# Sharing out one tensor's zeros among the transfer engines: another split of rows over GpSimd's and SP's transfers

## The chip, the cores and the metric

The kernel runs on one core of a Trainium2 chip. A core has TensorE for matrix products (PE; its weight loads are PEld), VectorE (DVE), ScalarE (ACT), GpSimd (POOL) and SyncE (SP), and sixteen transfer engines (DMA engines) that move data between the chip's memory and the core's SBUF, which has 128 partitions. The metric is the device time of one execution in microseconds. The kernel before took 272.31 us, the median of 3 runs (272.19 to 272.38).

## The reference

One decoding step of a transformer layer with its gradients: `x + attention(layernorm(x)) + ffn(layernorm(x))` for 4 batch rows with one token each, model width 512. The attention has 32 query heads and 8 key/value heads of 128; it looks only at the last `W = 1024` of `Sk = 4096` cached positions. The feed-forward part has a gate, an up and a down matrix with inner width 1792.

```python
xn = _layernorm(x)
k = k_cache[:, :, Sk - W:, :]        # each head used by 4 query heads; v likewise
p = softmax(einsum("bhqd,bhkd->bhqk", q, k) * Dh ** -0.5)
out = x + (p @ v).reshape(...) @ wo + (gelu(xn @ w_gate) * (xn @ w_up)) @ w_down
```

Nine outputs are wanted: `out`, and the gradients of x, of the two caches, and of five weight matrices, all in bf16. The gradients of the caches (out_2 and out_3) have the caches' full shape, 4 x 8 x 4096 x 128. Only the last 1024 positions of each head depend on the input; the first 3072 positions (`K0`) are zero, and the kernel has to write those zeros: 64 heads of 3072 x 128 elements, 50 MB of the 81 MB that it writes.

## The kernel before

**Zeros.** A tile `ztile` of 128 partitions by 6144 bf16 elements (12,288 bytes a partition, `ZW`) is set to zero once by GpSimd. A head's zero part is cut into 64 pieces (`ZP`) of 6144 elements, so that one row of `ztile` fills one piece. `zeros(n)` issues n transfers on SP's queue; each writes the zero parts of two heads (`ZG = 2`) with 128 pieces, from every other partition of `ztile`, 1.5 MB. There are 32 such pairs. A transfer of `zeros` waits for the one issued four earlier to have landed (`behind`, `deep=4`).

**One pair is written otherwise.** The last pair is taken off the list (`zog, zb, zg`) and written by `part_zeros`, with transfers that GpSimd issues. `part_zeros(m0, rows, each, part, after)` writes pieces m0 to m0 + rows * each of both heads. Its source has `rows` rows of `ztile`, the first in partition `part`; each row is read `2 * each` times. Three such transfers are issued while the second feed-forward weight gradient is prepared in program order; on GpSimd they come right behind a few fills, among the weight loads. They hold 15, 2 and 15 of the 64 positions. A fourth, with the other 32, is issued at the beginning of the last phase and waits for the zeros that SP issued last before it (`zdone[-1]`).

**Order of the work.** The weights come first, on SP's queue: gate, up, down, wq and wo. Then the feed-forward part and its gradients, then four rounds of attention, one for each batch row, then the last phase with the gradients of wo and wq, out and the gradient of x. SP's instructions stand in the order of the program (a `manual_schedule` for its engine); from the attention on TensorE, VectorE and ScalarE do too. GpSimd's instructions are placed by the scheduler, by what they depend on. SP's queue carries the loads, the results (`result`, from staging tiles) and the zeros, between which a list (`before`) says how many zeros go ahead of each result. SP's transfers use eight semaphores in turn, and each transfer waits for the one that used its semaphore before it, eight transfers back.

**Around the change.** After the feed-forward part SP issues the load of va, two zeros, the load of kb and four zeros.

Of the kernel before, what the change touches and what calls it, by code (L numbers as in the profile page):

```python
# [19 lines left out]
def kernel(  # L20
# [24 lines left out]
    nc = tc.nc  # L45
# [7 lines left out]
    K0 = Sk - W  # L53
# [29 lines left out]
    def evac(out, in_, n):  # L83

        ca, cd = (190 + n) / 1.2, (130 + n) / 0.96
        eng = "act" if load["act"] + ca <= load["dve"] + cd else "dve"
        load[eng] += ca if eng == "act" else cd
        if eng == "act":
            return nc.scalar.copy(out=out, in_=in_)  # L89
        return nc.vector.tensor_copy(out=out, in_=in_)  # L90

    def t32(out, in_, n):
        load["dve"] += (130 + n) / 0.96
        nc.vector.transpose(out=out, in_=in_)  # L94

    def pairs(ap):
        return ap.bitcast(U32)

    def scratch():
        return scrp.tile([P, 1024], U32, name="scr", tag="scr")  # L100
# [6 lines left out]
    def stg_tile():  # L107

        if not halves:
            pair = stg_pair()  # L110
            halves.extend(pair[:, h] for h in range(2))
        return halves.pop(0)
# [3 lines left out]
    def result(*parts):  # L116
        zeros(min(before.popleft(), len(ztodo)))
        for out, in_ in parts:
            nc.sync.dma_start(out=out, in_=in_)
# [19 lines left out]
    def mm(out, lhsT, rhs, first=True, last=True, pos=None):  # L139
        kw = {} if pos is None else {"tile_position": pos}  # L140
        nc.tensor.matmul(out, lhsT=lhsT, rhs=rhs, start=first, stop=last, **kw)  # L141

    def bank(name, tag="w", shape=(P, 512), dt=FP32):
        pool = {"w": ps_w, "x": ps_x}.get(tag, ps_a)
        return pool.tile(list(shape), dt, name=name, tag=tag)
# [75 lines left out]
    ZP = P // 2  # L221
    ZW = K0 // ZP * Dh
    ztile = const.tile([P, ZW], BF16, name="ztile")
# [36 lines left out]
    def window(dram, b, h):  # L260

        return dram[b, h * G // 2:(h + 1) * G // 2, K0:Sk, :].rearrange("g (m j) d -> m g (j d)", j=2 * J)

    def alternate(tl, h):

        t_ = tl[h:h + 1]
        return bass.AP(tensor=t_.tensor, offset=t_.offset,
                       ap=[[2 * t_.ap[0][0], P // 2], [2 * J * Dh, G // 2], [1, 2 * J * Dh]])

    def load_kv(b, k, pool, tag, eng, **kw):  # L270
        d_, src = ((k_t, A_k_cache), (v_t, A_v_cache))[k]
        tl = pool.tile([P, G // 2, 2 * J, Dh], BF16, name=tag, tag=tag)
        for h in range(2):
            with tc.high_priority():
                d = eng.dma_start(out=alternate(tl, h), in_=window(src, b, h), **kw)
        d_[b] = tl
        return d

    ZG = 2
    zsrc = bass.AP(tensor=ztile.tensor, offset=ztile.offset, ap=[[2 * ztile[:].ap[0][0], ZP], [0, ZG], [1, ZW]])  # L280
    ztodo = [(og, b, g) for b in range(B) for g in range(0, G, ZG) for og in (out_2, out_3)]
    zdone = []
    zog, zb, zg = ztodo.pop()

    def part_zeros(m0, rows, each, part, after=None):

        z = nc.gpsimd.dma_start(  # L287
            out=zog[zb, zg:zg + ZG, 0:K0, :].rearrange("g (m j) d -> m g (j d)", m=ZP)[m0:m0 + rows * each],
            in_=bass.AP(tensor=ztile.tensor, offset=ztile[part:part + 1, :].offset,
                        ap=[[4 * ztile[:].ap[0][0], rows], [0, ZG * each], [1, ZW]]))  # L290
        if after is not None:
            behind(z.ins, after.ins)

    def behind(ins, other):
        tc.add_manual_dep(ins, other.name,
                          mybir.DependencyInfo(mybir.DependencyClass.Sync, mybir.DependencyReason.DATA))

    def zeros(n, after=None, deep=4):

        for _ in range(n):  # L300
            og, b, g = ztodo.pop(0)
            z = nc.sync.dma_start(out=og[b, g:g + ZG, 0:K0, :].rearrange("g (m j) d -> m g (j d)", m=ZP), in_=zsrc)
            if len(zdone) >= deep:
                behind(z.ins, zdone[-deep].ins)
            if after is not None:
                behind(z.ins, after.ins)
            zdone.append(z)


    if True:  # L310
# [5 lines left out]
        def flat(t_):  # L316
            return t_[:].rearrange("p f c -> p (f c)")
# [92 lines left out]
        for wi, (wsb, dh, og) in enumerate(((wu_sb, dhu, out_7), (wg_sb, dhg, out_6))):  # L410
            dh_f = flat(dh)
            dhr = hgu[:].rearrange("p u f c -> p (u f c)").bitcast(BF16)
            for a, q in enumerate(quad):
                ps = bank("rep_ps", "w", (P, FQ))
                mm(ps[:], rsum_b[q, :], dh_f[q, :], pos=(Q * a, 0))
                evac(dhr[:, a * FQ:(a + 1) * FQ], ps[:], FQ)
            dhP = scratch()[:, 0:FPB * Q].rearrange("p (f x) -> p f x", f=FPB)
            t32(dhP, pairs(dhr[:, 0:F]), 896)
            dhs = ffn.tile([P, FPB, 2, 4 * B], BF16, name="dhs", tag=f"dhs{wi}")
            nc.gpsimd.memset(dhs[:], 0.0)  # L420
            if wi == 1:
                part_zeros(0, 3, 5, 0)
                part_zeros(15, 2, 1, 12)
                part_zeros(17, 3, 5, 20)
            dhPb = dhP.bitcast(BF16).rearrange("p f (x r) -> p f r x", r=2)
            for a, q in enumerate(quad):
                nc.vector.tensor_copy(out=dhs[q, :, :, a * B:(a + 1) * B], in_=dhPb[q, :, :, 0:B])
            for ch in range(4):
                sc = scratch()
                n7 = FPB // 4  # L430
                t32(sc[:, 0:n7 * P].rearrange("p (k c n) -> p c k n", k=n7, c=C),
                    pairs(wsb[:])[:, :, ch * n7 * Q:(ch + 1) * n7 * Q], 896)
                sb = sc[:, 0:n7 * P].bitcast(BF16).rearrange("p (k n r) -> p k r n", k=n7, r=2)
                for k in range(n7):
                    c = nm % 4
                    mm(dxf_ps[quad[c]].rearrange("p r n -> p (r n)"), dhs[:, ch * n7 + k].rearrange("p r x -> p (r x)"),
                       sb[:, k], nm < 4, nm >= 2 * FPB - 4, (0, Q * c))
                    nm += 1
            dwg_v = og.rearrange("(p h c) f -> h p (c f)", h=2, c=2)
            for h in range(2):  # L440
                stg = stg_tile()
                for ci in range(2):
                    for a, q in enumerate(quad):
                        ps = bank("dwg_ps", "w", (P, FQ))
                        mm(ps[:], xn_b[q, 2 * h + ci:D:C], dh_f[q, :], pos=(Q * a, 0))
                        o_ = (ci * NQ + a) * FQ
                        evac(stg[:, o_:o_ + FQ], ps[:], FQ)
                result((dwg_v[h], stg[:, 0:2 * F]))
# [4 lines left out]
    with tc.tile_pool(name="mid", bufs=1, reuse_waits="tile") as mid:  # L453
# [4 lines left out]
        with (tc.tile_pool(name="kvp", bufs=1, reuse_waits="tile") as kvp,  # L458
              tc.tile_pool(name="att", bufs=1, reuse_waits="tile") as att):
            load_kv(0, 1, kvp, "va", nc.sync)  # L460
            zeros(2)
            load_kv(1, 0, kvp, "kb", nc.sync)
            zeros(4)


# [2 lines left out]
            rows = [qm[:], dyBD[:].rearrange("p n r x -> p (n r x)").rearrange("p (b g d) -> p b g d", b=B, g=4)]  # L468
# [132 lines left out]
            def small(name, shape=(P, 1)):  # L601
                return att.tile(list(shape), FP32, name=name, tag=name)
# [72 lines left out]
            for b in range(B):  # L675
                S = sps[0][:]
                m = small("m")
# [124 lines left out]
            for i in range(KH):  # L802
                t, e, c = i // 8, i // 4 % 2, i % 4
# [12 lines left out]
            s_o = sums[:, 0:D]  # L816
            TT(out=s_o, in0=ob_ps[:], in1=fo[:], op=ALU.add)

            part_zeros(32, 8, 4, 64, zdone[-1])
            dwo_v = out_5.rearrange("(p t k) n -> t p (k n)", t=4, k=8)  # L820
            dwq_v = out_4.rearrange("(p c) j -> c p j", c=C)
            late = {}
# [126 lines left out]
```

## Time and profile before

| | |
|---|---|
| median of 3 runs | 272.31 us (272.19 to 272.38) |
| the profiled execution | 272.15 us |
| its span, first to last instruction | 270.4 us |
| DVE / PE / ACT / POOL busy | 67% / 61% / 51% / 13% of the span |
| last computation ends | about 243 us |
| moved | 111.9 MB, 414 GB/s over the span |
| HBM read, written | 30.7 MB, 81.0 MB |

Busy shares are of the span. A digit in a line of slices is the busy share of a fortieth of the span in tenths (9 is 90% or more). Queue q1 holds what SP issues, q0 what GpSimd issues. In the issues by line the columns are the target and source, the issuing engine, how many, the size of each, and the median time from issue to landing. The trace also has a record of every packet that a transfer engine moved: its queue, its size, its start and how long it took.

### The profile page before, as it was taken

How to read it: one execution, taken by the hardware profiler on the slowest of the kernel's cores; microseconds unless marked ns; L12 is line 12 of the kernel's file. 1: busy time of each engine (PE TensorE's matmuls, PEld its weight loads, DVE VectorE, ACT ScalarE, POOL GpSimd, SP SyncE). 2: the span in 40 equal slices, each digit the busy share in tenths (PEclk: the TensorE clock that was granted, in tenths of full speed). 3: DMA queues.
4: the chain of work that ended last, by engine and by line, in shares of the span. 5: the costliest groups of instructions: out<-in, count | busy, mean ns of one | idle time of the engine just before them, and what ended most of it. 6: DMA issues, size and time to landing. Idle time of an engine off the chain costs nothing.

```text
span 270.4 us, 3304 instructions
## 1 busy us (share of the span) xinstructions
PE 164.6 (61%) x1152; PEld 62.0 (23%) x1159; DVE 180.5 (67%) x339; ACT 137.4 (51%) x278; POOL 36.1 (13%) x95
## 2 busy tenths in 40 slices
PE   1256988968536687676568578585877898460000
PEld 0121342222112342123222233122421223010000
DVE  7869768978798428873588536793289999970000
ACT  2242775670022636696577765696476666460000
POOL 8900002091032101120012100000000000000000
PEclk9998885556855555997999975997577999555555
DMA  7999999999999999999999999999999999999994
GB/s 264 437 422 449 409 369 425 430 431 413 421 426 428 430 412 425 426 421 427 415 421 418 433 416 421 431 422 431 418 428 425 422 429 417 429 429 428 428 420 207
DMA packets 16640, 111.90 MB, mean 414 GB/s; under 512 B 1760, under 2 KB 1776, under 8 KB 10992
## 3 DMA queue, kind: packets, MB, share of 16 engines
q1 hardware_dynamic: 16072, 110.12, 97.7%
q0 software_dynamic: 544, 1.57, 1.5%
q8 instruction: 9, 0.15, 0.2%
q14 instruction: 7, 0.06, 0.1%
q10 hardware_dynamic: 8, 0.00, 0.0%
HBM read 30.68 MB, written 81.01 MB: 413 GB/s over the span
## 4 chain that ended last, share of the span: by engine, by line
DVE 21%; PE 21%; ACT 17%; issue 4%; ACTq 0%
DVE scr L94 9%; ACT stg L124 6%; ACT spr L584 5%; PE kv_ps L141 4%; PE dw_ps L141 4%; DVE stg L124 3%; PE sc_ps L141 3%; PE ok_ps L141 2%; DVE odt L647 2%; PE od_ps L141 2%; ACT late L124 2%; DVE dqs L763 2%; DVE wq_t L94 2%; PE ob_ps L141 1%; ACT last L124 1%
## 5 line engine op out<-in xcount | busy, mean ns | idle before, releaser
L124 ACT CAST stg<-kv_ps 128x512 bf16<-128x512 f32 x102 | 54.6, 598 | 26.5 <-PE kv_ps L141 26.4
L141 PE MATMUL sc_ps<-scr,bd 128*32 128x256 bf16 x256 | 20.1, 399 | 18.1 <-DVE scr L94 17.5
L141 PEld LDWEIGHTS <-spr 128*128 128x128 bf16 x256 | 17.0, 108 | 36.1 <-issue 24.3
L141 PE MATMUL kv_ps<-dyBD,spr 128*128 128x512 bf16 x60 | 24.1, 528 | 1.9 <-issue 1.3
L141 PE MATMUL kv_ps<-qm,spr 128*128 128x512 bf16 x63 | 19.7, 387 | 3.0 <-DVE stg L124 1.1
L94 DVE STREAM_TRANSPOSE scr<-va 128x1024 uint32<-128x1024 uint32 x16 | 19.5, 1224 | 0.0
L124 DVE CAST stg<-kv_ps 128x512 bf16<-128x512 f32 x10 | 6.6, 688 | 17.9 <-PE kv_ps L141 17.9
L89 ACT CAST stg<-dwg_ps 128x448 bf16<-128x448 f32 x26 | 12.0, 567 | 3.3 <-DMA out_dram<-stg 2.4
L549 POOL COPY bd<-D3q 32x64 bf16<-32x64 bf16 x32 | 7.6, 245 | 44.4 <-PE sc_ps L141 43.2
L141 PEld LDWEIGHTS <-bd 128*32 128x32 bf16 x256 | 6.3, 99 | 29.8 <-issue 27.2
L141 PE MATMUL dw_ps<-scr,xn_b 32*128 32x512 bf16 x32 | 9.4, 545 | 5.5 <-ACT late L124 4.0
L124 ACT CAST late<-dw_ps 128x512 bf16<-128x512 f32 x16 | 9.2, 588 | 6.8 <-PE dw_ps L141 6.7
L141 PE MATMUL do_ps<-scr,dyBD 128*128 128x512 bf16 x31 | 11.1, 491 | 2.3 <-DVE scr L94 1.9
L584 ACT ACTIVATE spr<-dS_b,amask 64x256 bf16<-64x256 bf16 x16 | 7.4, 554 | 8.5 <-DVE dS_b L728 8.5
L549 POOL COPY bd<-D3d 32x64 bf16<-32x64 bf16 x32 | 7.4, 239 | 31.7 <-PE sc_ps L141 16.4
L647 DVE SCALAR_TENSOR_TENSOR odt<-od_ps,om,odt 128x128 f32<-128x128 f32 x12 | 4.2, 351 | 11.1 <-ACT odt L642 10.8
L124 DVE CAST stg<-dw_ps 128x512 bf16<-128x512 f32 x16 | 10.5, 685 | 1.5 <-PE dw_ps L141 1.3
L287 POOL DMA_DIRECT2D out_dram<-ztile x4 | 3.0, 753 | 61.9 <-DMA out_dram<-ztile 61.9
L94 DVE STREAM_TRANSPOSE scr<-wo_sb 128x1024 uint32<-128x1024 uint32 x8 | 9.8, 1237 | 1.6 <-PE do_ps L141 1.0
L124 ACT CAST stg<-dw_ps 128x512 bf16<-128x512 f32 x16 | 8.9, 588 | 3.6 <-PE dw_ps L141 3.4
L94 DVE STREAM_TRANSPOSE scr<-ka 128x1024 uint32<-128x1024 uint32 x8 | 9.8, 1233 | 1.2 <-PE r_ps L141 1.1
L124 DVE CAST late<-dw_ps 128x512 bf16<-128x512 f32 x16 | 10.4, 675 | 0.3 <-PE dw_ps L141 0.3
(203 smaller groups left out, 337.4 us busy)
## 6 DMA issues: line engine op xcount, KB each, us to landing
out_dram<-ztile SPq DMA_DIRECT2D x31, 1536.0 KB, 19.1
out_dram<-stg SPq DMA_DIRECT2D x18, 1024.0 KB, 14.7
va<-in_A_v_cache_dram SPq DMA_DIRECT2D x8, 1024.0 KB, 14.3
out_dram<-stg SPq DMA_DIRECT2D x6, 896.0 KB, 11.9
wq_sb<-in_A_wq_dram SPq DMA_DIRECT2D x1, 4096.0 KB, 27.9
wo_sb<-in_A_wo_dram SPq DMA_DIRECT2D x1, 4096.0 KB, 37.3
ka<-in_A_k_cache_dram SPq DMA_DIRECT2D x4, 1024.0 KB, 15.6
kb<-in_A_k_cache_dram SPq DMA_DIRECT2D x4, 1024.0 KB, 19.0
```

The costliest lines, as they stand in the source:

```text
L89: return nc.scalar.copy(out=out, in_=in_)
L94: nc.vector.transpose(out=out, in_=in_)
L124: return nc.scalar.copy(out=out, in_=in_) if eng == "act" else nc.vector.tensor_copy(out=out, in_=in_)
L141: nc.tensor.matmul(out, lhsT=lhsT, rhs=rhs, start=first, stop=last, **kw)
L287: z = nc.gpsimd.dma_start(out=zog[zb, zg:zg + ZG, 0:K0, :].rearrange("g (m j) d -> m g (j d)", m=ZP)[m0:m0 + rows * each], in_=bass.AP(ten ...
L549: nc.gpsimd.tensor_copy(out=t_[q, :, :, g2, :, o_:o_ + 4], in_=src[q, b, g2])
L584: nc.scalar.activation(out=out, in_=in_, func=ACT.Copy, scale=amask[q, a:a + 1])
L647: STT(out=t_[:], in0=ps[:, g, :], scalar=(om, oms)[k][:, g:g + 1], in1=t_[:], op0=ALU.mult, op1=ALU.add)
L763: nc.vector.tensor_copy(out=dqs[q, :, :, :, a * B + b], in_=d3v[q])
```

## The change

The two heads that GpSimd wrote with 15 + 2 + 15 positions early and 32 late are split another way. GpSimd writes 5 positions from 5 rows (one position each), and 32 from 8 rows (4 each), issued where the three transfers were. In the last phase there are two `part_zeros` in place of one: 12 positions from 3 rows that start in partition 104, with the same wait as before, and 12 from 3 rows that start in partition 0, with no wait given. Rows of the source now lie eight partitions apart instead of four. The last 3 positions of both heads are written by SP, in a new function `rest_zeros`: 16 rows of 2304 elements, from one partition in eight, issued behind the load of kb. The target is written through a view (`zpart`) with the head as its outer dimension.

```diff
+    zpart = zog[zb, zg:zg + ZG, 0:K0, :].rearrange("g (m j) d -> g m (j d)", m=ZP)
+
     def part_zeros(m0, rows, each, part, after=None):
 
         z = nc.gpsimd.dma_start(
-            out=zog[zb, zg:zg + ZG, 0:K0, :].rearrange("g (m j) d -> m g (j d)", m=ZP)[m0:m0 + rows * each],
+            out=zpart[:, m0:m0 + rows * each].rearrange("g m e -> m g e"),
             in_=bass.AP(tensor=ztile.tensor, offset=ztile[part:part + 1, :].offset,
-                        ap=[[4 * ztile[:].ap[0][0], rows], [0, ZG * each], [1, ZW]]))
+                        ap=[[8 * ztile[:].ap[0][0], rows], [0, ZG * each], [1, ZW]]))
         if after is not None:
             behind(z.ins, after.ins)
+
+    def rest_zeros(m0):
+
+        n = (ZP - m0) * ZW // 8
+        nc.sync.dma_start(out=zpart[:, m0:ZP].rearrange("g m e -> g (m e)").rearrange("g (k e) -> g k e", k=8),
+                          in_=bass.AP(tensor=ztile.tensor, offset=ztile.offset, ap=[[8 * ztile[:].ap[0][0], 16], [1, n]]))
...
             if wi == 1:
-                part_zeros(0, 3, 5, 0)
-                part_zeros(15, 2, 1, 12)
-                part_zeros(17, 3, 5, 20)
+                part_zeros(0, 5, 1, 0)
+                part_zeros(5, 8, 4, 40)
...
             load_kv(1, 0, kvp, "kb", nc.sync)
+            rest_zeros(61)
             zeros(4)
...
-            part_zeros(32, 8, 4, 64, zdone[-1])
+            part_zeros(37, 3, 4, 104, zdone[-1])
+            part_zeros(49, 3, 4, 0)
```

## The prediction

> **What bounds the kernel now.** The page's slices come first, for the share of time in which the 16 transfer engines move data.
>
> ```profile
> DMA  7999999999999999999999999999999999999994
> GB/s 264 437 422 449 409 369 425 430 431 413 421 426 428 430 412 425 426 421 427 415 421 418 433 416 421 431 422 431 418 428 425 422 429 417 429 429 428 428 420 207
> DMA packets 16640, 111.90 MB, mean 414 GB/s; under 512 B 1760, under 2 KB 1776, under 8 KB 10992
> q1 hardware_dynamic: 16072, 110.12, 97.7%
> q0 software_dynamic: 544, 1.57, 1.5%
> ```
>
> The engines are full in all but the first and last slice. Then the table by stage (length, busy time of PE, PEld, DVE, ACT and POOL, granted clock, DMA share, GB/s):
>
> ```profile
> 42.00:100.00 58.00, 39.43 (x258) 14.62 (x252) 43.49 (x72) 23.08 (x48) 15.48 (x43) 0.56 1.01 425
> 100.00:200.00 100.00, 68.78 (x541) 29.11 (x545) 63.86 (x133) 67.06 (x143) 7.96 (x32) 0.83 1.02 423
> 200.00:243.00 43.00, 32.80 (x205) 8.78 (x204) 40.52 (x66) 28.54 (x54) 0.65 (x1) 0.81 1.02 426
> 243.00:266.00 23.00, 0.00 (x0) 0.00 (x0) 0.00 (x0) 0.00 (x0) 0.00 (x0) 0.50 1.00 424
> ```
>
> From 243 us nothing computes any more and the transfers need another 26 us. The end is that of the transfer engine that finishes last. So the question is what each engine has to move. The issues by line show the changed transfers:
>
> ```profile
> out_dram<-ztile SPq DMA_DIRECT2D x31, 1536.0 KB, 19.1
> out_dram<-ztile POOLq DMA_DIRECT2D x1, 768.0 KB, 11.9
> out_dram<-ztile POOLq DMA_DIRECT2D x2, 360.0 KB, 25.1
> out_dram<-ztile POOLq DMA_DIRECT2D x1, 48.0 KB, 21.9
> ```
>
> The packet records of the trace have no engine number. I chained each packet to the one that begins as it ends (within some 4 ns), backward from the last one, holding each chain to the order in which SP's queue must come. It gives 16 chains without an idle stretch over 0.3 us back to 30 us. The transfers that use only some engines name them: x, out_0 and out_1 (four rows) use engines 0 to 3; GpSimd's four take the engines in turn, as many as they have source rows: 0-2, 3-4, 5-7 and 8-15. Packets of 12,288 B (one piece) per engine and the end of its last packet:
>
> - engines 0-2: 10 pieces, 267.2 to 267.6 us
> - engine 3: 2 pieces, 265.1
> - engine 4: 2 pieces, 268.9; its packets are slower all the way (476 ns a piece, where the rest take 460)
> - engines 5-7: 10 pieces, 266.6 to 267.7
> - engines 8-15: 8 pieces, seven at 266.5 to 266.9, and one at 268.9, which brought two of PE's nine 16 KB instruction packets and a slow stretch at 34 us
>
> The mean is 267.0, so two of the sixteen, engine 4 and one of 8-15, set the end.
>
> **The change, part by part.** All of it moves packets between engines; 128 pieces stay 128. The sum is made on the profiled execution, 272.15 us (span 270.4, the rest lies around it), 0.16 under the median of 272.31.
>
> Early zeros. Before: 10, 2 and 10 pieces on engines 0-2, 3-4, 5-7. After: the 5 rows put 2 pieces on each of engines 0-4, and the 8 rows put 8 on each of 5-12. The engines go on in turn from there.
>
> Late zeros. Before: 8 pieces on each of 8-15, behind a landed SP transfer. After: two transfers of 3 rows by 8. Only the first has that wait. The compiled order on GpSimd shows that the second, which has none, stands third among the weight loads, so that it goes to engines 13-15, early; the one left at the end goes to engines 0-2. Which engine carries what is as it would be without that, as they are taken in turn, so I cost the place at nothing; the cover is a transfer system with no idle stretch after 30 us.
>
> SP's 16 rows. 16 packets of 4,608 B. By the rows between which it lies, 4,096 B at 159 ns and 7,168 B at 272 ns, one takes 178 ns, about 175 in a chain. How many engines share them isn't shown for SP: its transfers of 64 or 128 rows on both sides use 16 engines, four rows use four. GpSimd's, with 15 rows at the target and 3 at the source, use 3, the number that divides both. Here the source has 16 rows and the target's outer dimension is 2. I take two engines (0 and 1), eight packets each, 8 x 175 = 1.40 us; the other end is one packet for each of sixteen, 0.18 us. [...]
>
> So per engine, at 457 ns a piece in a chain:
> - 0, 1: 10 pieces as before, + 1.40 us: 268.6 to 269.0
> - 2: 10, unchanged, under 267.6; 3 and 4: 2, unchanged, 265.1 and 268.9
> - 5-7: 10 to 8, -0.91 us: 265.7 to 266.8
> - 8-15: 8, unchanged: 266.5 to 266.9 and 268.9
>
> The last was 268.93 and is now 268.93 to 268.96: +0.0 us. With sixteen engines instead of two everyone gets 0.18 us more but 5-7, and the end is +0.2 us. The engines that get relief weren't last.
>
> SP's queue gets one more issue, between the loads of kb (65.4 us) and four zeros. An issue there took 0.3 to 2.0 us and the transfers behind it began 14 us after their issue, so it is hidden. Each SP transfer waits for the one eight before it, and the small one takes one place of eight for some 20 us. Behind it wait four zeros, then the next va. The least lead of any issue over the first packet it feeds is 2.1 us (at 172 us), in that stretch 3.5 us (va at 93 us); without that cover engines would run dry. I expect more lead: the lightest engines then carry 2 pieces instead of 0 and the heaviest 8 instead of 10.
>
> Weight loads. They share the engines with the early zeros. The heaviest gets 8 pieces instead of 10, so wo should land about 0.9 us earlier and wq some 2 us earlier (fewer pieces fall among its eight packets). If the first small transfer starts sooner, among wd's packets, it delays wd by up to 2 x 0.46 = 0.9 us. Neither reaches the end: the transfers finish 26 us after the last computation.
>
> Sum: 272.15 + 0.0 to 0.2; on the median's scale 272.3 to 272.5. I say **272.4 us**.
>
> **Rivals.**
>
> *Two engines on one group of rows (slower).* The source is now one row in eight partitions (0, 8, ... 120) where it was one in four, engines 8-15 reading partitions 64 to 92. If partitions are reached by groups that serve one engine at full rate, engines 0-2 read at the end from groups (104, 112, 120) which others are draining for SP's transfers. A piece then takes up to double: 8 x 0.46 = 3.7 us on engines 0 and 1 and on their partners, 276.0; with half of the packets meeting, 274.2. It decides as soon as one piece in seven meets another (0.5 us). Against it: every piece of the old kernel, GpSimd's 64 late ones too, takes 460 to 481 ns; but there nothing shows two engines at one group. [...] No row here can tell. Chance 0.2.
>
> *Engines 0 and 1 are made the last (slower).* With 13 shares they stand beside engine 4 at 268.6 to 269.0. The slow stretch of 33 to 36 us, in which weight packets take 1.4 to 2.1 us instead of 1.21, cost engines between 0.2 and 1.6 us. If it falls on 0 or 1, which had about 0.35 of it, the end moves by up to 1.2 us: 273.0 as the middle. Chance 0.15.
>
> *The two last engines are late only in this execution (faster).* If in most runs engine 4 and the other one aren't late, engines 5-7 are the last, and 0.91 us goes from them. Engines 0-2 come next, 0.1 us behind; spread over sixteen, SP's packets give them 0.18 us, so that up to 0.9 us stays gained where they are further behind: 271.4 at best, 271.7 in the middle. With two engines the 1.40 us take it back. Against it: three runs lie within 0.2 us of one another, as a lateness that comes and goes would not let them. Chance 0.2.
>
> *The change doesn't do what it says.* It doesn't, in the two places named (12 pieces early instead of late; two engines perhaps instead of sixteen); both are in the sum.
>
> **How the numbers follow.** 0.2% is 0.54 us, about what a measurement of this kernel can tell from no change. The likeliest, with its own range 271.9 to 272.8, has 0.45, and all of it is "same". The two slower rivals have 0.35, the faster one 0.2. The range, 271.5 to 274.3, leaves out the outer part of the faster rival and of the first slower one, under 0.2 together.
>
> **What would show it.** In the changed profile: q0 with 122 pieces, 1.50 MB; q1 with 16 packets of 4,608 B and 2 completions more (16,090), 16 completions more (16,104) if it is spread. DMA at 9 in all slices between the first and the last. Chains with 2, 8 and 13 shares as above, engine 4 among the last. wq and wo landing earlier. Wrong would be: late GpSimd pieces near 900 ns (the first rival); an engine 0 or 1 alone last by over 0.5 us (the second); a last packet before 268.4 (the third); an idle stretch after 42 us (the leads).

## Result and the profile after

The changed kernel is slower: 276.64 us median of 6 runs (275.82 to 277.78) against 272.25 (271.93 to 274.59) for the kernel before on the same chips. The ratio is 1.0151, with a 95% interval of 1.0107 to 1.0194, so 2.9 to 5.3 us more. The forecast was 272.4 and no change. The execution profiled took 275.95 us, its span is 274.2.

Slices and queues of the page of the changed kernel:

```profile
DMA  7999999999999999999999999999999999999992
GB/s 269 435 401 433 448 384 402 427 427 421 414 420 425 425 420 423 426 422 422 415 391 418 426 420 421 428 419 434 412 437 418 432 380 414 432 424 428 423 396 116
DMA packets 16594, 111.90 MB, mean 408 GB/s; under 512 B 1704, under 2 KB 1720, under 8 KB 10952
q1 hardware_dynamic: 16090, 110.19, 96.9%
q0 software_dynamic: 480, 1.50, 1.4%
```

The engines are busy in every inner slice, as before, and the bytes are the same. The mean over the whole span fell from 414 to 408 GB/s. As the slices stay full, nothing ran dry; packets took longer. One slice stands out, the 33rd (219 to 226 us), with 380 GB/s where the old kernel had 429. The table by stage cuts closer (length, busy time of PE, PEld, DVE, ACT and POOL, granted clock, DMA share, GB/s). First the stretch from 217 to 228 us in the kernel before:

```profile
217.00:228.00 11.00, 10.17 (x108) 3.46 (x101) 9.85 (x17) 7.11 (x13) 0.00 (x0) 1.00 1.01 419
```

And the changed kernel:

```profile
42.00:100.00 58.00, 39.38 (x259) 14.55 (x260) 43.68 (x72) 23.02 (x48) 15.43 (x43) 0.56 1.01 422
100.00:200.00 100.00, 66.61 (x548) 27.79 (x552) 66.78 (x137) 69.14 (x150) 8.15 (x32) 0.89 1.02 420
217.00:228.00 11.00, 9.89 (x93) 3.59 (x93) 9.78 (x19) 7.49 (x14) 0.00 (x0) 1.00 1.00 392
243.00:266.00 23.00, 0.00 (x0) 0.00 (x0) 0.00 (x0) 0.00 (x0) 0.00 (x0) 0.50 1.00 423
266.00:274.20 8.20, 0.00 (x0) 0.00 (x0) 0.00 (x0) 0.00 (x0) 0.00 (x0) 0.50 0.35 147
```

Two losses show. From 217 to 228 us, when the late GpSimd pieces move, the rate is 392 against 419 at the same share of busy time. And over 42 to 200 us it is 422 and 420 where it was 425 and 423: little, but over 158 us. From 243 to 266 us the rates agree (423 and 424). The last 8 us run at a share of 0.35: engines finish one after another.

Two sums say how much. **Stretch**: for each data packet, the time it took beyond the usual time of its size (159 ns for 4,096 bytes, 460 ns for 12,288), added up over all sixteen engines. **End spread**: the last transfer that uses all sixteen engines reports sixteen completions, one for each engine (265.4 to 269.4 us in the kernel before, each 0.3 to 0.5 us behind the end of a chain of packets); their mean says how much time the engines needed on average, their maximum when the slowest was done.

| kernel (profiled execution) | stretch 42-200 us | stretch 217-228 us | mean completion | last completion | late pieces: mean, max ns |
|---|---|---|---|---|---|
| before | 14.5 | 1.3 | 267.4 | 269.4 | 461, 481 |
| after | 31.9 | 12.3 | 269.2 | 273.2 | 555, 1105 |

The stretch grew by 17.4 + 11.0 = 28.4 us, which over sixteen engines is 1.8 us; the mean completion moved by 1.8 us. So stretched packets account for the rise of the mean, to some 0.3 us: outside these two stretches the sum changed by a few us more. The other 2.0 us of the last completion's 3.8 come from how unevenly this falls.

The chains of packets, made as for the prediction, say on whom. The last are three of engines 8-15, which end at 272.9, 271.6 and 271.5 us; each was stretched by 2.7 to 3.1 us between 220 and 230 us. The packets that stretched there are SP's zeros: between 217 and 230 us, 21 of SP's pieces of 12,288 bytes took over 520 ns, up to 969, and one (521 ns) in the kernel before. Engines 0 to 2 follow at 271.0, 270.8 and 270.0.

### The profile page after: what moved, and what is told of

Read it like the earlier page. It is cut to its first block, busy times and chain, and to the rows that moved or that the text cites. A ratio compares the mean times of both kernels' runs of the same rounds, so it can differ in the third digit from the quotient of the medians.

```text
span 274.2 us, 3304 instructions
## 1 busy us (share of the span) xinstructions
PE 162.2 (59%) x1152; PEld 59.9 (22%) x1159; DVE 180.9 (66%) x339; ACT 136.8 (50%) x278; POOL 35.9 (13%) x95
## 3 DMA queue, kind: packets, MB, share of 16 engines
q1 hardware_dynamic: 16090, 110.19, 96.9%
## 4 chain that ended last, share of the span: by engine, by line
PE 20%; DVE 17%; ACT 15%; DMA 6%; issue 3%; SPq 0%; ACTq 0%; DVEq 0%
DVE scr L94 7%; DMA va<-in_A_v_cache_dram 6%; ACT stg L124 5%; ACT spr L592 5%; PE kv_ps L141 4%; PE dw_ps L141 4%; DVE stg L124 2%; PE od_ps L141 2%; PE sc_ps L141 2%; ACT late L124 2%; DVE wq_t L94 2%; DVE odt L655 2%; PE ok_ps L141 1%; PE ob_ps L141 1%; DVE dqs L771 1%
## 5 line engine op out<-in xcount | busy, mean ns | idle before, releaser
L141 PE MATMUL sc_ps<-scr,bd 128*32 128x256 bf16 x256 | 20.1, 399 | 18.7 <-DVE scr L94 18.1
L141 PEld LDWEIGHTS <-spr 128*128 128x128 bf16 x256 | 16.4, 105 | 35.6 <-issue 22.1
L141 PE MATMUL kv_ps<-dyBD,spr 128*128 128x512 bf16 x60 | 21.6, 474 | 1.9 <-issue 1.3
L141 PE MATMUL kv_ps<-qm,spr 128*128 128x512 bf16 x63 | 20.9, 413 | 2.3 <-DVE stg L124 1.1
L124 DVE CAST stg<-kv_ps 128x512 bf16<-128x512 f32 x10 | 6.6, 688 | 14.9 <-PE kv_ps L141 14.9
## 6 DMA issues: line engine op xcount, KB each, us to landing
out_dram<-stg SPq DMA_DIRECT2D x18, 1024.0 KB, 16.1
wq_sb<-in_A_wq_dram SPq DMA_DIRECT2D x1, 4096.0 KB, 26.8
wo_sb<-in_A_wo_dram SPq DMA_DIRECT2D x1, 4096.0 KB, 37.5
kb<-in_A_k_cache_dram SPq DMA_DIRECT2D x4, 1024.0 KB, 19.9
```

The source lines that it names most:

```text
L124: return nc.scalar.copy(out=out, in_=in_) if eng == "act" else nc.vector.tensor_copy(out=out, in_=in_)
```

## Experiments

Times are medians; ratios are against the kernel before on the same chip, with a 95% interval. The other columns are from one profiled execution of each kernel, in us unless marked ns:

| kernel | time, us | ratio | stretch 42-200 | stretch 217-228 | mean, last completion | late pieces: mean, max ns |
|---|---|---|---|---|---|---|
| b_src0 | 275.05 | 1.0098 [1.0055, 1.0141] | 17.3 | 37.1 | 270.3, 271.8 | 705, 1069 |
| b_src96 | 272.65 | 1.0003 [0.9975, 1.0031] | 13.3 | 1.3 | 267.3, 269.6 | 460, 460 |
| b_near | 282.82 | 1.0373 [1.0298, 1.0447] | 16.8 | 50.4 | 273.2, 279.7 | 1667, 3051 |
| a_own | 274.40 | 1.0059 [1.0031, 1.0088] | 29.3 | 0.5 | 268.4, 271.5 | 460, 460 |
| a_norest | 275.58 | 1.0113 [1.0072, 1.0155] | 30.5 | 13.1 | 269.2, 272.7 | 602, 1096 |
| a_own_nr | 273.91 | 1.0047 [1.0022, 1.0072] | 36.6 | 0.5 | 268.7, 271.8 | 460, 460 |
| a_late | 275.52 | 1.0102 [1.0053, 1.0152] | 26.1 | 14.9 | 269.1, 272.0 | 570, 1051 |
| b_none | 275.46 | 1.0102 [1.0047, 1.0157] | 26.0 | 36.0 | 268.7, 272.8 | 631, 1079 |
| b_two | 274.71 | 1.0072 [1.0047, 1.0097] | 29.6 | 1.3 | 267.1, 271.5 | 463, 547 |
| b_pairs | 278.95 | 1.0246 [1.0198, 1.0293] | 50.5 | 2.9 | 272.2, 275.5 | 474, 825 |

Names with b change the kernel before, names with a the changed one. The first theory was that of the first rival: two engines read one group of partitions at once. Its rival was that the split itself, with 13 shares on engines 0 and 1, sets the end.

**Only the source rows moved, in the old kernel (b_src0, b_src96, b_near).** Engines, pieces and targets stay; only the partitions that the last transfer reads change.

```diff
# b_src0
-            part_zeros(32, 8, 4, 64, zdone[-1])
+            part_zeros(32, 8, 4, 0, zdone[-1])
# b_src96
+            part_zeros(32, 8, 4, 96, zdone[-1])
# b_near: rows one partition apart, 64 to 71, instead of four
+            part_zeros(32, 8, 4, 64, zdone[-1], step=1)
```

> The kernel before with one number changed: GpSimd's last transfer (engines 8-15, 8 pieces each) reads partitions 0, 4, ... 28 instead of 64, 68, ... 92; the split of pieces over the engines is that of before. Shared rows (an engine that reads from a group of partitions which another engine is draining takes half its rate): engines 8-15 now read the groups of engines 0-7, whose packets of 12,288 bytes between 217 and 228 us stretch by some 3 us in sum on each; engine 4, last already at 268.9, ends near 272, and the time is 275 to 276 us. The split of the pieces (13 shares on engines 0 and 1, or the early places): nothing of that is here, 272.3 us.

> The kernel before, with GpSimd's last transfer reading partitions 96, 100, ... 124 instead of 64, 68, ... 92. Shared rows, with partitions 32 apart in one group: each engine still reads its own group, nothing stretches, 272.3 us. Shared rows, with groups of neighbouring partitions only: the rows belong to other engines, some engines stretch by 3 us, 274 to 276 us. The split of the pieces: 272.3 us.

> The kernel before with GpSimd's last transfer reading partitions 64, 65, ... 71 instead of 64, 68, ... 92: its eight engines now share two groups of four partitions. Shared rows, a group serving about one engine's rate (12,288 bytes in 0.46 us): 32 pieces, 14.7 us, go through each of two groups beside what engines 8 and 9 take from them; late pieces take up to five times 0.46 us, and the last engine ends some 8 to 15 us later, 280 to 287 us. Only rows that belong to another engine cost, whatever their group: at most what the rows at 0 to 28 cost, 275 us. The split of the pieces: 272.3 us.

All three came as the theory said. The table by stage of b_src0:

```profile
100.00:200.00 100.00, 69.94 (x538) 27.91 (x538) 63.54 (x133) 65.87 (x143) 7.89 (x32) 0.80 1.02 423
217.00:228.00 11.00, 10.32 (x107) 3.40 (x107) 9.63 (x16) 7.08 (x14) 0.00 (x0) 1.00 1.00 331
243.00:266.00 23.00, 0.00 (x0) 0.00 (x0) 0.00 (x0) 0.00 (x0) 0.00 (x0) 0.50 1.01 423
```

Of b_src96:

```profile
217.00:228.00 11.00, 10.52 (x80) 3.40 (x79) 7.53 (x13) 5.92 (x11) 0.00 (x0) 0.60 1.01 421
```

And of b_near:

```profile
217.00:228.00 11.00, 10.29 (x99) 3.23 (x99) 8.92 (x16) 6.59 (x13) 0.00 (x0) 0.87 1.04 315
228.00:243.00 15.00, 9.25 (x38) 2.56 (x37) 13.65 (x29) 9.01 (x17) 0.00 (x0) 0.61 0.99 354
```

With the same sixteen engines at about the same busy share, 331 or 315 GB/s move instead of 419 while the late pieces are under way (in b_near up to 237 us, with another 36 us of stretch from 228 to 243 us), and elsewhere the rate is nearly unchanged. Rows 0 to 28 read by engines 8-15 cost 36 us of stretch more, over sixteen engines 2.2 us, and the median rose by 2.3. Rows 96 to 124 cost nothing beside 64 to 92. From rows 64 to 71 a piece takes 1667 ns on average, 3.6 times the usual, and the 64 pieces took 18.4 us (218.7 to 237.1). So the rows that a late piece is read from set what it takes: 461 ns on average from rows 64 to 92, 460 from 96 to 124, 705 from 0 to 28 (1.5 times) and 1667 from 64 to 71. The groups of the theory are an estimate from these runs: 3.6 times fits four engines on each of two groups of four rows, as one engine alone would need 32 x 0.46 = 14.7 of the 18.4 us for 32 pieces, and 460 ns fits rows 96 to 124 in the groups of 64 to 92. Where a group begins and ends, and which other rows belong to it, no run shows.

Not every meeting costs. Early in the changed kernel, partitions 64 and 96, which the theory puts in one group, are two of the eight rows (40, 48 ... 96) that GpSimd's second transfer reads on eight engines. It moves its pieces in rounds of eight. In the round from 18.7 to 19.6 us they start within 0.42 us of one another, so that any two of them overlap, and each takes 460 ns; none of the 98 early pieces took more than 467. There each engine moves a weight packet of 1.2 us between two pieces, while in the last phase all engines read SBUF without a pause (DMA share 1.00 from 217 to 228 us). That this pause is the reason is not shown.

**The changed kernel, with the late rows of engines 0-2 moved to those that they read early in the kernel before (a_own).** These three engines read partitions 0, 4 and 8 instead of 104, 112 and 120.

```diff
-            part_zeros(37, 3, 4, 104, zdone[-1])
+            part_zeros(37, 3, 4, 0, zdone[-1], step=4)
```

> The changed kernel with the source of GpSimd's last transfer (3 rows by 8, engines 0-2) at partitions 0, 4 and 8 instead of 104, 112 and 120; all else as changed. Shared rows: the three engines of 8-15 that end last in the changed kernel (271.5 to 272.9 us) no longer stretch between 217 and 228 us and end 3 us or more earlier; the last are engines 0, 1 and 4, and the time falls from 276.6 to 272.5 to 273.5 us. Engines 0 and 1 made the last by their 13 shares: the load is the same, so the time stays within 0.7 us of 276.6.

The time fell to 274.40, its late pieces take 460 ns again, and the rate of that stage is back:

```profile
42.00:100.00 58.00, 40.07 (x257) 14.90 (x253) 43.32 (x72) 23.02 (x48) 15.42 (x43) 0.56 1.01 422
100.00:200.00 100.00, 69.12 (x542) 28.48 (x541) 63.23 (x131) 66.77 (x143) 7.89 (x32) 0.85 1.02 420
217.00:228.00 11.00, 10.13 (x87) 2.08 (x84) 7.61 (x13) 5.67 (x11) 0.00 (x0) 0.50 1.01 420
```

By the ratios this takes 2.5 of the 4.1 us away, the largest part. But 1.6 us (0.8 to 2.4) stay, and 274.40 is above the 272.5 to 273.5 that the theory gave: there is a second cause, and the first two rows show where, 422 and 420 GB/s as in the changed kernel.

**SP's 16 rows left out (a_norest, a_own_nr).** Both leave the last 3 positions of the two heads unwritten; the second is a_own without them.

```diff
             load_kv(1, 0, kvp, "kb", nc.sync)
-            rest_zeros(61)
             zeros(4)
```

> The changed kernel without SP's 16 rows: the last 3 positions of the two heads are not written. Engines 0 and 1 have 1.4 us less to move. Shared rows: three engines of 8-15 are the last, so nothing changes beyond 0.4 us: 276.2 to 276.9 us. Engines 0 and 1 made the last by their 13 shares: the time falls by 1.0 to 1.4 us, to about 275.4 us.

> The changed kernel with its last transfer reading partitions 0, 4, 8, and without SP's 16 rows (3 positions of two heads not written). With the stretch at the end gone, engines 0 and 1 are last at 271.2 and 270.8 us, and one other at 270.9. The 13 shares on engines 0 and 1: 0.3 to 0.8 us less than with the rows, about 273.8 us. If SP's rows cost through their place in its queue instead, loads stretch less as well, and the time falls by 1.2 us or more.

a_own_nr is 0.5 us faster than a_own by the medians, 0.3 by the ratios (they were measured on two chips), in line with 1.40 us less on engines 0 and 1, which in a_own are among the last (271.2 and 270.8 us). The intervals overlap, so it isn't resolved. a_norest, at 275.58, lies between the two values expected, nearer to the 275.4 of the 13 shares; by the ratios it is 1.0 us faster than the changed kernel, again with overlapping intervals, and its mean completion is the same (269.2). Neither brings the time back to the old kernel's: SP's rows are worth 0.3 to 1.0 us by these runs, which none of them resolves.

**Both late transfers behind the wait (a_late).** This puts the second one, which the compiled order had moved among the weight loads, back to the end.

```diff
-            part_zeros(49, 3, 4, 0)
+            part_zeros(49, 3, 4, 0, zdone[-1])
```

> The changed kernel with the same wait on both late transfers, so that the 12 positions stand at the end as written: first those from partitions 104, 112, 120, on engines 13-15, then those from 0, 8, 16, on engines 0-2. Shared rows: engines 13-15 read what engines 10, 12 and 14 drain, and engines 1 and 2 what 2 and 4 drain, so that five engines more than their own stretch by 2 to 3 us; engine 4, which is slow, is one of them: 276 to 278 us, no better than the changed kernel. The place of the second transfer as the cause: 272.3 to 273 us.

It stays slow, at 275.52, with 570 ns a late piece: a little below the 276 to 278 expected from shared rows, and well above the 272.3 to 273 of the place as the cause. Its point estimate is below the changed kernel's 276.64, but that was measured in another group of runs and the intervals overlap. So the early place isn't the main cause; a small part of its own can't be told here, since by the theory both late transfers now read from groups that other engines use. Which engine uses which of these rows, as the expectation has it, no run shows.

**What remains: the loads in the middle.** The extra 15 to 17 us of stretch in 42-200 us (after, a_own) lie in packets of 4,096 bytes: 8.1 us before, 24.6 after. Loads of the caches and results for the caches' gradients both have this size; told apart by their order in SP's queue, the loads went from 5.0 to 22.5 us (19.7 in a_own) and the results from 3.1 to 2.1. It is few packets: 106 of 7,056 took over 30 ns longer than usual, 44 of these over 200 ns longer; before, it was 38 and 16 of 7,043. The early split goes with it: the four kernels with the old one (before, b_src0, b_src96, b_near) have 13.3 to 17.3 us of stretch there, the eight with another, those below included, 26.0 to 50.5.

GpSimd moves no piece from 42 us (in b_pairs below, 50 us) until the last phase. What differs is how the engines stand. By the sixteen completions of one load, at 45 to 51 us, they lie apart by 4.9 us in the old kernel, as those with 10 early pieces are behind the rest; in the changed one by 4.3, but ten of them stand within 0.6 us. The second theory: engines that stand level meet in the loads more. Three kernels were made for it from the old one, without SP's 16 rows.

```diff
# b_none: no early pieces (32 of 64 positions of both heads unwritten)
-                part_zeros(0, 3, 5, 0)
-                part_zeros(15, 2, 1, 12)
-                part_zeros(17, 3, 5, 20)
# b_two: 2 early pieces on each of engines 0-7, from rows 0 to 28 (24 positions unwritten)
+                part_zeros(0, 8, 1, 0)
# b_pairs: GpSimd writes four heads, SP one pair less: 20, 4, 20 early and 16 late pieces an engine
+    ztodo.remove((zog, zb, zg - ZG))
+    zg, ZH = zg - ZG, 2 * ZG
...
-                        ap=[[4 * ztile[:].ap[0][0], rows], [0, ZG * each], [1, ZW]]))
+                        ap=[[4 * ztile[:].ap[0][0], rows], [0, ZH * each], [1, ZW]]))
```

> The kernel before without GpSimd's three early transfers; 32 of the 64 positions of the two heads are not written, 4.6 us of work less on each of engines 0-2 and 5-7, none on 8-15. All engines then run level through the attention. Engines side by side stretch each other's loads of the caches (4,096-byte packets): the stretch between 42 and 200 us, 14 us over all engines in the kernel before, grows to 25 us or more, and the time rises above 273 us, although there is less to write. Loads stretch for another reason: 10 to 18 us of stretch, and the time stays at 272.3 us, set by the one engine of 8-15 that ended last before.

> The kernel before with its three early transfers replaced by one of 8 rows, one position each: 2 pieces on each of engines 0-7, from their own rows; 24 of the 64 positions of the two heads are not written. The last transfer is on engines 8-15 with its own rows as before. Engines 8-15 have exactly the work of before, 0-2 and 5-7 have 3.7 us less, 3 and 4 the same; nothing shares rows. Level engines stretch each other's loads: through the attention all engines stand within 1 us, the stretch between 42 and 200 us grows from 14.5 us to 25 us or more, and the time does not fall though there is less to write: 272.8 to 274 us. No such effect: 13 to 18 us of stretch, and 271.5 to 272.3 us.

> The kernel before with four heads instead of two written by GpSimd, from the same rows: 20, 4 and 20 pieces early on engines 0-2, 3-4 and 5-7, 16 late on 8-15, and one of SP's zeros less (8 pieces less on every engine). Engines then stand 9 us apart through the attention instead of 4.6. Level engines stretch each other's loads: further apart they stretch less, 14 us or less between 42 and 200 us; the last are engines 0-2 and 5-7 at about 268.5 and the one of 8-15 at 268.9 us, 272.3 us, if the lightest engines do not run dry (the least lead of an issue was 2.1 us); if they do, the transfer share drops below 9 in some slices and the time is 273 to 275 us. No such effect: stretch as before, 272.3 us.

b_none had a flaw: in the kernel before GpSimd's four transfers take the engines in turn (0-2, 3-4, 5-7, 8-15), and by that order the late one, without the early three, falls to engines 0-7. They then read rows 64 to 92, and a late piece takes 631 ns on average. Its time says nothing of the second theory (36.0 us of stretch in 217-228 us); the stretch in 42-200 us does, with 26.0 us, 16.7 of it in loads.

b_two is clean. Its late pieces are the old kernel's, on the same engines, at 463 ns:

```profile
42.00:100.00 58.00, 39.05 (x257) 13.89 (x258) 44.16 (x73) 22.63 (x48) 15.47 (x43) 0.56 1.01 422
100.00:200.00 100.00, 67.97 (x548) 28.76 (x553) 65.85 (x137) 68.14 (x148) 8.21 (x32) 0.87 1.02 421
217.00:228.00 11.00, 10.16 (x99) 3.42 (x100) 9.63 (x19) 7.71 (x14) 0.00 (x0) 1.00 1.01 419
```

It moves 48 pieces less, which over sixteen engines is 48 x 0.46 / 16 = 1.4 us less; yet the mean completion is only 0.3 us earlier, since packets stretched 15.1 us more in 42-200 us (0.9 us an engine; the loads went from 5.0 to 19.9 us), and the last completion is 2.1 us later. Taking work from engines 0-2 and 5-7 made the kernel 0.7% slower (0.5 to 1.0), and at 274.71 it is above even the 272.8 to 274 expected. That is shown, and neither shared rows nor SP's 16 rows are in it.

But the theory in its simple form falls with b_pairs, in which the engines stand twice as far apart (9.7 us). Its loads should have stretched less, and they stretch most: 29.4 us of the 50.5, where 14 or less were expected in all, and the time is 278.95. a_late speaks against it too: there the engines lie 4.7 us apart, about as in the old kernel, and the stretch is 26.1 us, 16.1 of it in loads. The page of b_pairs, DMA share and rate, and two rows of its table by stage:

```profile
DMA  7999999999999999999999999999999999999993
GB/s 281 431 442 413 391 391 420 412 423 357 371 417 428 428 414 420 424 422 424 416 413 415 429 420 417 409 377 426 412 424 421 412 426 417 422 426 418 425 393 159
42.00:100.00 58.00, 36.50 (x227) 12.99 (x226) 42.02 (x68) 20.84 (x44) 15.46 (x43) 0.57 1.00 408
100.00:200.00 100.00, 70.48 (x552) 29.09 (x556) 62.19 (x130) 66.52 (x143) 8.22 (x32) 0.76 1.01 416
```

The engines don't run dry either; the tenth and eleventh slices (62 to 76 us) have 357 and 371 GB/s at 9. Nor does the number of load packets under way at once order the kernels: between 42 and 108 us, 15 to 17 of them were under way for 51 of 2075 packets in the old kernel, for 1105 of 2030 in the changed one and for 1 of 1821 in b_pairs (two records of one engine overlap by 3 ns, so that the count can pass 16). So the split of the early pieces changes the stretch in 42-200 us, by 12 to 36 us over all engines, most of it in loads; why is open. Not tested is the side of the memory: the heads that one load reads lie 1 MB apart there, the records carry no address, and no run changed the order of a load. None of these kernels is faster than the old one.

## Why the prediction was wrong

**What bounds the kernel: right.** The end is that of the transfer engine that finishes last, in every run; in the changed kernel nothing computes behind 243 us either.

**The shares: right.** q0 has 122 pieces and 1.50 MB, q1 16,090 packets, so that SP's 16 rows went to two engines (two chains of eight packets of 178 ns, at 85 us), as the number that divides both sizes had it, read from GpSimd's transfers (3 engines for 15 and 3 rows). The second late transfer stands among the weight loads, for engines 13-15. The leads hold: no idle stretch after 42 us. wq landed 1.1 us earlier (26.8 us from its issue, 27.9 before), where some 2 were forecast; wo, forecast 0.9 us earlier, did not (37.5, 37.3 before). Neither reaches the end.

**Late zeros, wrong: "so I cost the place at nothing".** The sum asked which engine carries a piece and not which rows it reads, and took 457 ns a piece for all. The late pieces took 555 ns on average and up to 1105. That is the first rival's step, "Two engines on one group of rows", with its price: it gave 274.2 to 276.0. It had 0.2 and should have had more. The 276.64 measured lies above even this price, as a second loss came on top. The reason against it, that every old piece took 460 to 481 ns, was no evidence: in the old kernel the late source rows lie where they cost nothing, and rows 96 to 124 (b_src96, 460 ns a piece) do too, but rows 0 to 28 (b_src0, 705 ns) don't. b_src0 is that kernel with this alone changed, and it loses 2.3 us.

**A size in that rival was off.** It doubled the piece on engines 0 and 1 and "their partners" alike. Here engines 0 to 2, which read rows 104, 112 and 120, were stretched by only some 0.7 us each, and three of engines 8-15 by 2.7 to 3.1.

**"The lightest engines then carry 2 pieces instead of 0 and the heaviest 8 instead of 10", wrong in what it brings.** The step saw levelling as a gain in leads and put no cost on it. With another split of the early pieces, packets between 42 and 200 us stretched by 17.4 us more, 1.1 us an engine, nearly all of it in the loads of the caches. No term and no rival held this. b_two shows the cost without the other two effects; why it arises is open.

**Engines 0 and 1 with 13 shares: the second rival, small.** In a_own, where no rows are shared, they end at 271.2 and 270.8 us, among the last, and leaving the 1.40 us out gains 0.3 to 0.5 us, not resolved; in a_norest it is 1.0 us by the ratios, not resolved either.

**The gain of engines 5-7 and the third rival** (two engines late only in one execution): not met. The old kernel's medians lie between 272.2 and 272.8 us in the four groups of runs, and b_src96, with the same shares, has the same late end (269.6). But the reason given against it, three runs within 0.2 us, was luck: single runs of that kernel lie between 271.9 and 274.8 us.

The sum, by ratios: 2.5 us from shared rows (4.1 less 1.6), 0.3 from SP's rows, 1.3 from the stretched loads. Each of the three is known to about 1 us.

## What to carry to other kernels

Where transfers set the time, ask of each not only which engine moves a piece but from which partitions it reads, and who else reads there while the engines read without a pause: in b_src0 the rows alone took the rate from 419 to 331 GB/s. The code gives a table of source partitions by engine, once the chains of packets show how many engines a transfer uses. A split that keeps the sum and relieves only engines that aren't last had nothing to gain here, and it cost. "Every packet took its usual time so far" is no reason against contention if in the old code, as here at 460 to 481 ns a piece, no packets slowed each other.

## What was not expected of the hardware

In the changed kernel's last phase both sides were slowed, and not by the same: engines 0 to 2, which read rows 104, 112 and 120, by 0.7 us each, three of engines 8-15 by 2.7 to 3.1. The rate of all sixteen engines shows it at an unchanged busy share (392 for 419 GB/s, and 331 in b_src0), so the share alone, at 9 in all slices, hides it.

The split of GpSimd's early pieces, over by 42 us, changes the rate of the next 158 us by about 0.7% (422 and 420 for 425 and 423 GB/s), and 0.59 MB less to write made the kernel slower by 2.0 us (b_two).

Most packets of GpSimd's queue carry no piece. The old kernel's q0 has 544 packets: 128 pieces, and 416 of 4 bytes. The 416 fit 4 x 16 completions and, on each engine that a transfer leaves out, as many packets of 4 bytes as one of the transfer's own engines moves pieces: 10 x 13 + 2 x 14 + 10 x 13 + 8 x 8 = 352. In the changed kernel, with 480 packets, the other 358 fit in the same way: 64 + 2 x 11 + 8 x 8 + 8 x 13 + 8 x 13.
